# Attention and two feed-forward layers on one core: score jobs that share banks, one job for both products with v, transposes of full width, and another opening

## The chip, the cores and the metric

One core of a Trainium2 chip runs the whole program. The metric is the device time of one execution in microseconds (us), taken as a median of several runs. Five engines work side by side, each through its own list of instructions in order: TensorE (PE, with its weight loads PEld), VectorE (DVE), ScalarE (ACT), GpSimd (POOL) and SyncE (SP), which issues nearly all DMA transfers. TensorE writes into eight PSUM banks of 128 x 512 floats, and VectorE and ScalarE empty them.

## The reference

Four batches of eight heads, 576 positions of 64 numbers:

```
scores = q @ k.T / 8                         (per head, 576 x 576)
cum    = cumsum(log(clip(f, 1e-4, 1)))       (per head, 576)
scores = where(above the diagonal, -1e9, scores + cum[i] - cum[j])
attn   = softmax(scores);  x = attn @ v      -> x: 2304 tokens x 512
h = x @ w_in;   g = h * clip(h + 3, 0, 6) / 6;   x2 = g @ w_out      (512 -> 2048 -> 512)
h = x2 @ w_in2; g = softplus(h);                 out = g @ w_out2
```

## The kernel before

**Stages.** The four big products of the two feed-forward layers run one after the other. The first (step_g, "G", line 965) runs beside the attention, the other three (step_c line 1213, step_a line 1069, step_b line 1268) run alone, on seven products instead of eight of half size. A float32 value is split there in a high and a low part of TensorE's faster type, so one product is three matmuls. The matmuls of the attention are plain float32.

**Attention.** Two heads make a pair; there are 16 pairs, four to a batch. For each pair:

- Raw q and k come by DMA in the tiles qr and kr (load_qk, line 527), and VectorE turns them (qk_job, line 563). For the very first pair this is done head by head.
- decays() computes the running sum of log f for all heads, stores a scaled copy to dec_dram (lines 770, 771), and each later pair gets its two rows broadcast to 128 partitions in the tiles w (line 568). The first pair's rows are spread by TensorE (first_decays, line 583). GpSimd then writes a large number above the diagonal of each 128-wide block of w (hide, line 624).
- The queries are cut in five tiles, CUT: tile 0 has 64 rows, the tiles 1 to 4 have 128, and tile t needs as many key columns as its last row. s_job (line 609) is one **score job** ("S"): the matmuls of one row of S_JOBS for both heads. Five jobs a pair; tiles 1 and 0 share a bank, tile 4 takes two jobs.
- VectorE adds w to the scores out of the bank, takes the row minimum (least, line 631) and writes the tile p; ScalarE takes the exponential and its sum (line 640).
- inv_job takes the inverse of all ten sums at once (lines 654, 655) and scales the ten tiles (fit, line 662).
- t_job (line 690, "T") turns 128 x 128 blocks of p, four jobs a head, one bank each; blocks of tile 0 are 64 rows high and give 64 columns. ScalarE copies the bank to the tiles pt (line 712).
- pv_job (line 737, "V") multiplies with v; two jobs, one for the query columns 320 to 576 and one for 0 to 320, one bank each. ScalarE and VectorE write the result as high and low part (lines 749, 750) into MX, where G reads it.

The pairs' tiles are in two sets (index z), the probabilities in four (p, pb, pc, pd).

**What sets the order.** Nothing is scheduled by the hardware. The program first records every piece of work (op) with its cost, its due time `at` and what it reads and writes; Work.order then plays the engines forward with those costs, gives each engine the ready piece with the least due time, deals out the banks, and emits the instructions in that order. The due times come from the table PLAN. G matmuls are thus dealt in between S, T and V, three or more at a time. Both first-layer weights and later ones pass through staging tiles st: loaded (line 843), converted by ScalarE and VectorE (lines 863 to 867), split (lines 947, 948). The first such load waits for the stored decays (`["dec"]` in weights_g).

The core of the score job:

```python
for ti, a, c, o, q0, r, y, lead, last in todo:
    for h in heads:
        nc.tensor.matmul(bank[bks[h, y].i][:, o:o + c - a], T["Q"][z][h * D:h * D + D, q0:q0 + P],
                         T["K"][z][h * D:h * D + D, a:c], start=lead, stop=last, skip_group_check=True)
```

Of the kernel before, what the change touches and what calls it, by code (L numbers as in the profile page):

```python
# [13 lines left out]
P = 128  # L14
# [6 lines left out]
S_JOBS = [[[(4, 0, 288)]], [[(4, 288, 576)]], [[(3, 0, 448)]], [[(2, 0, 320)]], [[(1, 0, 192), (0, 0, 64)]]]  # L21
# [30 lines left out]
    pc=658.575,  # L52
    pp=2838.384,
    pv=205.16,
    bend=[0.997, 1.008, 0.963, 0.815],
    b0=46.727,
    T0=62.991,
    D1=93.866,
    D2=78.328,
    D3=63.878,  # L60
    D4=62.724,
    gap=14.813,
    gap2=18.0,
    gap3=23.877,
    cA=1.049,
    SA=4.93,
    SC=5.336,
    SB=2.063,
    iva=12.955,
    nwarm=18,  # L70
    sp=0.252,
    evb=0.144,
    u0=8.176,
    u1=53.717,
    u2=4.715,
    u3=-39.214,
    fx=-1.569,
    ul=20.0,
    c1=53.569,
    c2=18.268,  # L80
    c3=11.259,
    cvw=0,
    ldw=91.154,
    xa=26.079,
    xs=-4.984,
    ga=1.976,
    tsp=-12.9,
    fit=7.316,
    xat=22.311,
    xl=4.236,  # L90
    rel=29.77,
    wfrom=5.061,
    lv0=9.944,
    lq1=16.782,
    decst=4.817,
    capH=5,
    capA=7,
    eps=0,
    slp=0,
    slv=0,  # L100
    lat=2.539,
# [16 lines left out]
class Work:  # L118
# [45 lines left out]
    def order(self, caps, eps, slack, lat):  # L164
# [9 lines left out]
        ham = {"w": 0, "act": {}, "warm": False}  # L174

# [42 lines left out]
        while len(out) < len(ops):  # L218
            best = None
            for e in self.ENGINES:  # L220
# [24 lines left out]
                _, s, o = min((c for c in cand if c[0] <= low + eps), key=lambda c: (c[2].at, c[0]))  # L245
# [5 lines left out]
            cost = next(wy[1] for wy in o.ways if wy[0] == e)  # L251
            for wy in o.ways:
                ready[wy[0]].remove(o)
# [48 lines left out]
def attention_two_moe_kernel(  # L302
# [188 lines left out]
    op(("pool", 500, lambda: make_identity(nc, ident)), w=["ident"])  # L491
    op(("dve", 8, lambda: nc.vector.memset(half, 0.5)), w=["half"])
# [22 lines left out]

    def load_qk(nm, b, hp, at, heads=(0, 1)):

        wk.mark = ()
        src = {"qr": q, "kr": k}[nm]

        first = nm == "kr" and (b, hp) == (0, 0)
        eng = nc.scalar if first else nc.sync

        def go():
            for h in heads:
                for g in range(0, D, 32):
                    eng.dma_start(
                        out=raws[nm][h * D + g:h * D + g + 32].rearrange("s (n d) -> s n d", d=32),
                        in_=src[b, 2 * hp + h, :, g:g + 32].rearrange("(n s) d -> s n d", s=32),
                    )  # L530

        n = len(heads)
        dma(go, n * S * D * 4 * 2, 2 * n, 560.0, "act" if first else "sp", w=[(nm, h) for h in heads], at=at, name="load " + nm, from_=at - K["rel"])
# [21 lines left out]
    def qk_job(b, hp, nm, at):  # L555
# [5 lines left out]
        for hs in [(0,), (1,)] if pn == 0 else [(0, 1)]:  # L561
            a, c = hs[0] * D, hs[-1] * D + D
            op(("dve", 726.0, lambda a=a, c=c: nc.vector.transpose(T[x][z][a:c], raws[nm][a:c])), part=(a, a),
               r=[(nm, h) for h in hs], w=[(x + "T", z, h) for h in hs], at=at - (pn == 0 and a == 0), name="T" + x)
# [24 lines left out]

    def s_job(pn, i, idx, at):  # L590
# [7 lines left out]
        need = [(x, z, h) for x in ("QT", "KT") for h in heads]  # L598
        todo = []
# [6 lines left out]
        def go():  # L606
            for ti, a, c, o, q0, r, y, lead, last in todo:
                for h in heads:
                    nc.tensor.matmul(  # L609
                        bank[bks[h, y].i][:, o:o + c - a], T["Q"][z][h * D:h * D + D, q0:q0 + P], T["K"][z][h * D:h * D + D, a:c],  # L610
                        start=lead, stop=last, skip_group_check=True,
                    )

        cost = sum(1.667 * (x[2] - x[1]) + 12 for x in todo) + 200
        op(("pe", cost, go), rows=0.8, seq="S",
           r=need, w=list(bks.values()), banks=list(bks.values()), at=at, name=f"S{pn}.{i}{idx}",
           after=[("P", sets[h], x[0]) for x in todo for h in heads])
        for ti, a, c, o, q0, r, y, _, _ in todo:
            for h in heads:
                par, bk = sets[h], bks[h, y]  # L620
                if c == q0 + r:
# [25 lines left out]
    def inv_job(pn, at):  # L647
# [5 lines left out]
        def inv():  # L653
            nc.vector.tensor_scalar(iv[pn % 2], sv[:, 1], 1e-9, None, op0=ALU.add)
            nc.vector.reciprocal(iv[pn % 2], iv[pn % 2])

        op(("dve", 340, inv), r=[("st", pn % 2, h, t) for h in range(2) for t in range(n)], w=[("iv", pn % 2)], at=at, name="inv")
        for h in range(2):
            for t, (q0, r) in list(enumerate(CUT))[::-1]:
# [4 lines left out]
                op2(("dve", dve(q0 + r, True), fit), r=[("iv", pn % 2)], w=[("P", set_of(pn, h), t)], at=at + 0.1 * (4 - t) + h * K["fit"], name=f"fit{t}")  # L664

    def t_job(pn, i, idx, at):
# [19 lines left out]
        def go():  # L686
            acc = bank[bk.i]
            for p0, ti, k0 in blocks:
                r = CUT[ti][1]
                nc.tensor.transpose(acc[:, p0:p0 + r], T["P"][par][ti][0:r, k0:k0 + P], ident[0:r, 0:r])  # L690

        op(("pe", sum(109.0 if CUT[b[1]][1] == P else 55.0 for b in blocks), go), r=list(rd), w=[bk], banks=[bk], at=at, name=f"TP{idx}",
# [26 lines left out]
    def pv_job(b, hp, idx, at):  # L719
        pn = b * HP + hp  # L720
        z = pn % 2
        y = z
        wk.mark = ()
        bk = Bank(att_banks, "a")
        a, c = V_JOBS[idx]
        rd = [("vr", z)]
        for jobs in T_JOBS:
            for j, ta, tcc in jobs:
                if ta < c and tcc > a:
                    rd += [("PT", i, j, ta - KCUT[j][0]) for i in range(2)]  # L730
        todo = [(i, j, max(a, KCUT[j][0]) - KCUT[j][0]) for j in V_ORDER[idx] for i in range(2)]

        def go():
            acc = bank[bk.i]
            for n, (i, j, s) in enumerate(todo):
                k0 = KCUT[j][0]
# [674 lines left out]
```

## Time and profile before

| | us |
|---|---|
| median of 3 runs | 949.13 |
| lowest and highest run | 947.28, 950.8 |
| the profiled execution, its own time | 948.23 |
| its span, first to last instruction | 946.4 |
| TensorE busy | 927.0 (98%) |
| VectorE busy | 733.3 (77%) |
| ScalarE busy | 538.0 (57%) |
| GpSimd busy | 110.0 (12%) |

The mean granted TensorE clock is 0.993 of full speed. The page's chain of work that ended last, followed back from the end, is 90% TensorE. Stages by time: attention with G from the start to 331 us, G alone to 403, then step_c to 583, step_a to 762 and step_b to the end. A busy TensorE is not one at its peak: matmul ends are modelled, and matmuls overlap. How long a job really holds the engine is read from the chain of waits, whose pieces follow one another without overlap.

### The profile page before, as it was taken

How to read it: one execution, taken by the hardware profiler on the slowest of the kernel's cores; microseconds unless marked ns; L12 is line 12 of the kernel's file. 1: busy time of each engine (PE TensorE's matmuls, PEld its weight loads, DVE VectorE, ACT ScalarE, POOL GpSimd, SP SyncE). 2: the span in 40 equal slices, each digit the busy share in tenths (PEclk: the TensorE clock that was granted, in tenths of full speed). 3: DMA queues.
4: the chain of work that ended last, by engine and by line, in shares of the span. 5: the costliest groups of instructions: out<-in, count | busy, mean ns of one | idle time of the engine just before them, and what ended most of it. 6: DMA issues, size and time to landing. Idle time of an engine off the chain costs nothing.

```text
span 946.4 us, 18694 instructions
## 1 busy us (share of the span) xinstructions
PE 927.0 (98%) x6756; PEld 824.4 (87%) x6756; DVE 733.3 (77%) x1696; ACT 538.0 (57%) x1090; POOL 110.0 (12%) x241
## 2 busy tenths in 40 slices
PE   5999999999999999999999999999999999999998
PEld 4666766777677788899999999999999999999998
DVE  7878977766777468688898799978645888888785
ACT  5868866666677555443354355777567754333332
POOL 3322221111111011102002102100001100000000
PEclk9999999999999999999999999999999999999999
DMA  9957768788666688444534365798624544543442
GB/s 185 184 143 171 208 170 215 203 230 222 173 214 206 200 283 281 155 151 147 172 111 156 113 181 174 267 369 303 240 101 156 190 155 133 154 133 117 133 135 67
DMA packets 196973, 172.76 MB, mean 183 GB/s; under 512 B 103504, under 2 KB 147792, under 8 KB 196880
## 3 DMA queue, kind: packets, MB, share of 16 engines
q1 hardware_dynamic: 194512, 171.27, 61.6%
q8 instruction: 53, 0.87, 0.4%
q10 hardware_dynamic: 2368, 0.30, 0.3%
q14 instruction: 40, 0.33, 0.1%
HBM read 111.68 MB, written 59.84 MB: 181 GB/s over the span
## 4 chain that ended last, share of the span: by engine, by line
PE 90%; DVE 3%; DMA 3%; issue 2%; POOL 1%; ACT 1%; DVEq 0%; POOLq 0%; ACTq 0%
PE bank L965 22%; PE bank L1268 19%; PE bank L1213 19%; PE bank L1069 15%; PE bank L690 6%; PE bank L609 5%; PE bank L737 4%; DMA st<-in_moe_w_out_dram 1%; DMA g_dram<-HY 1%; DMA st<-in_moe_w_in_dram 1%; DMA w<-dec_dram 0%; DVE p L662 0%; DMA wf_dram<-st 0%; POOL w L624 0%; DMA st<-wf_dram 0%
## 5 line engine op out<-in xcount | busy, mean ns | idle before, releaser
L1268 PE MATMUL bank<-U,MX 128*128 128x256 f32 x1512 | 179.9, 281 | 0.0
L1268 PEld LDWEIGHTS bank<-U,MX 128*128 128x128 f32 x1512 | 179.6, 189 | 0.0
L965 PE MATMUL bank<-MX,U 128*128 128x512 f32 (+1 forms) x768 | 177.5, 376 | 0.0
L1213 PE MATMUL bank<-XO,U 128*128 128x256 f32 x1344 | 159.3, 280 | 0.0
L1213 PEld LDWEIGHTS bank<-XO,U 128*128 128x128 f32 x1344 | 158.5, 189 | 0.1
L965 PEld LDWEIGHTS bank<-MX,U 128*128 128x128 f32 x768 | 124.8, 188 | 25.1 <-issue 4.4
L1069 PE MATMUL bank<-MX,U 128*128 128x288 f32 x672 | 91.5, 296 | 0.1
L1069 PE MATMUL bank<-XO,U 128*128 128x288 f32 x672 | 91.2, 296 | 0.0
L1069 PEld LDWEIGHTS bank<-MX,U 128*128 128x128 f32 x672 | 90.2, 188 | 0.5 <-ACT HY L1085 0.3
L1069 PEld LDWEIGHTS bank<-XO,U 128*128 128x128 f32 x672 | 90.3, 188 | 0.0
L624 POOL TENSOR_SCALAR_AFFINE_SELECT w<-w 128x128 f32<-128x128 f32 (+1 forms) x160 | 54.9, 348 | 224.3 <-DVE stats L631 149.5
L970 ACT ACTIVATE HY<-bank,half 128x512 f32<-128x512 f32 x80 | 50.7, 643 | 53.2 <-PE bank L965 46.0
L1166 ACT ACTIVATE MX<-GR 128x768 fp32r<-128x768 f32 x36 | 30.4, 845 | 86.8 <-PE bank L1268 50.4
L971 DVE SCALAR_TENSOR_TENSOR HY<-HY,bank 128x512 f32<-128x512 f32 x80 | 49.5, 628 | 35.3 <-ACT HY L970 34.8
L1088 DVE TENSOR_TENSOR HY<-HY,bank 128x288 f32<-128x288 f32 x96 | 43.1, 451 | 40.1 <-PE bank L1069 39.0
L712 ACT ACTIVATE pt<-bank 128x448 f32<-128x448 f32 (+2 forms) x128 | 59.7, 498 | 21.4 <-PE bank L690 19.8
L1085 ACT ACTIVATE HY<-bank 128x288 f32<-128x288 f32 x128 | 50.6, 408 | 35.8 <-PE bank L1069 34.8
L1166 ACT ACTIVATE XO<-GR 128x768 fp32r<-128x768 f32 x36 | 30.4, 843 | 67.4 <-PE bank L1213 45.1
L609 PE MATMUL bank<-KT,QT 64*128 64x288 f32 (+4 forms) x384 | 59.4, 419 | 6.8 <-DVE stats L631 3.6
L1170 DVE TENSOR_TENSOR MX<-GR,MX 128x768 fp32r<-128x768 f32 x36 | 34.4, 957 | 29.5 <-ACT MX L1166 29.5
L609 PEld LDWEIGHTS bank<-KT,QT 64*128 64x128 f32 x384 | 32.1, 185 | 28.1 <-issue 10.4
L938 DVE TENSOR_TENSOR U<-st,U 128x1024 fp32r<-128x1024 f32 (+1 forms) x48 | 53.6, 1130 | 3.8 <-ACT U L935 3.8
(153 smaller groups left out, 1454.8 us busy)
## 6 DMA issues: line engine op xcount, KB each, us to landing
GR<-g_dram SPq DMA_DIRECT2D x72, 512.0 KB, 3.8
g_dram<-HY SPq DMA_DIRECT2D x32, 576.0 KB, 3.6
st<-in_moe_w_in_dram SPq DMA_DIRECT2D x32, 512.0 KB, 4.8
g_dram<-HY SPq DMA_DIRECT2D x64, 256.0 KB, 3.2
st<-in_moe_w_out_dram SPq DMA_DIRECT2D x32, 512.0 KB, 5.2
wf_dram<-st SPq DMA_DIRECT2D x48, 256.0 KB, 3.6
st<-wf_dram SPq DMA_DIRECT2D x48, 256.0 KB, 3.1
w<-dec_dram SPq DMA_DIRECT2D x30, 288.0 KB, 5.0
```

Of the source, the lines that this page charges most:

```text
L609: nc.tensor.matmul(bank[bks[h, y].i][:, o:o + c - a], T["Q"][z][h * D:h * D + D, q0:q0 + P], T["K"][z][h * D:h * D + D, a:c], start=lead, ...
L624: nc.gpsimd.affine_select(out=blk, in_=blk, compare_op=ALU.is_ge, fill=-1e9 / scale, base=0, pattern=[[-1, r]], channel_multiplier=1)
L690: nc.tensor.transpose(acc[:, p0:p0 + r], T["P"][par][ti][0:r, k0:k0 + P], ident[0:r, 0:r])
L712: e.activation(out=place(i, j, a, c), in_=src(), func=ACTF.Copy)
L938: e.tensor_tensor(to(1), src(), to(0).bitcast(F32), op=ALU.subtract)
L965: nc.tensor.matmul(bank[bk.i][:, 0:n], w, x, start=(c == 0 and y == 0), stop=(c == NC - 1 and y == 2))
L970: op(("act", act(n, True, 1) + 10, lambda: nc.scalar.activation(out=g, in_=bank[bk.i][:, 0:n], func=ACTF.Relu, scale=1.0 / 6.0, bias=half) ...
L1069: nc.tensor.matmul(bank[bks[b].i][:, 0:HA], wa[u][:, c], xa[v][:, c], start=(nm in ("P1", "P2", "P5") and c == 0 and y == 0), stop=(c == 1 ...
L1085: op(("act", act(HA, True) + 30, lambda: nc.scalar.activation(out=to(q), in_=bp(), func=ACTF.Copy)), r=new, banks=[ba], w=[("H", i, q)], a ...
L1166: op(("act", act(cnt, False), lambda src=src, dst=dst: nc.scalar.activation(out=dst(0), in_=src(), func=ACTF.Copy)), r=rd, w=[("gf", m, i, ...
L1213: nc.tensor.matmul(bank[bks[b].i][:, o * 256:(o + 1) * 256], *ops, start=(p == 0 and o == 0 and y == 0), stop=(p == NPR - 1 and y == 2), s ...
L1268: nc.tensor.matmul(bank[bks[b].i][:, o * 256:(o + 1) * 256], ga[u], wa[v], start=(p == 0 and o == 0 and y == 0), stop=(p == NPR - 1 and y ...
```

## The change

- **Score jobs share banks.** S_JOBS has four jobs instead of five: tile 0 goes into tile 3's bank, tile 1 into tile 2's. Tile 0's minimum is taken after the next job (late_rows).
- **They stand together.** Work.order gets a bonus `stick`: after a score job or a product with v, TensorE prefers another of the same kind; it also charges each change of kind on TensorE (`turn`).
- **One job for both products with v**, with two banks.
- **Transposes of full width**: blocks of tile 0 are turned with all 128 rows (64 of them zeros), and the next block overwrites the surplus columns.
- **First masks by TensorE**: for the first pair the large number is added by matmuls of the identity with a tile `bar`, ten in all, and GpSimd's ten selects on w fall away.
- **Raw q, k and decays sooner**: the second pair's q and k land in two tiles p that are still free, so they need not wait for the first pair's; the first sum of decays is due sooner; weights no longer wait for it.
- For the first four pairs the inverse is taken in two parts, tiles 3 and 4 first.
- Nearly every number of PLAN is another one. They are due times, margins and penalties, and no work.

```diff
-S_JOBS = [[[(4, 0, 288)]], [[(4, 288, 576)]], [[(3, 0, 448)]], [[(2, 0, 320)]], [[(1, 0, 192), (0, 0, 64)]]]
+S_JOBS = [[[(4, 0, 288)]], [[(4, 288, 576)]], [[(3, 0, 448), (0, 0, 64)]], [[(2, 0, 320), (1, 0, 192)]]]
...
-    capH=5,
+    capH=4,
-    slp=0,
+    slp=139.65,
+    stick=11.647,
...
+                same = last if e == "pe" and last in ("S", "V") else ""
+                _, s, o = min((c for c in cand if c[0] <= low + eps), key=lambda c: (c[2].at - (stick if same and kind_of(c[2]) == same else 0.0), c[0]))
...
+    bar = ap.tile([P, P], F32, name="bar")
+    op(("pool", 346, lambda: nc.gpsimd.affine_select(out=bar, in_=bar, compare_op=ALU.is_ge, fill=-1e9 / scale, base=0, pattern=[[-1, P]], channel_multiplier=1)), w=["bar"])
...
+    def raw(nm, pn, heads):
+        if pn == 1:
+            y = 2 + (nm == "kr")
+            return T["P"][y][4][:, 0:S], [("P", y, 4)]
+        return raws[nm], [(nm, h) for h in heads]
...
+            for ti, a, c, o, q0, r, y, lead, last in todo if barred else ():
+                if c == q0 + r:
+                    for h in heads:
+                        nc.tensor.matmul(bank[bks[h, y].i][:, o + q0 - a:o + c - a], ident, bar[:, 0:r], start=False, stop=last, skip_group_check=True)
...
+        if idx == 2:
+            late_rows.append(rest.pop())
+        elif idx == 3:
+            rest.append(late_rows.pop())
...
+        for t0, t1 in ((3, n), (0, 3)) if pn < 4 else ((0, n),):
...
-                nc.tensor.transpose(acc[:, p0:p0 + r], T["P"][par][ti][0:r, k0:k0 + P], ident[0:r, 0:r])
+                nc.tensor.transpose(acc[:, p0:p0 + P], T["P"][par][ti][:, k0:k0 + P], ident)
...
-        bk = Bank(att_banks, "a")
-        a, c = V_JOBS[idx]
+        bks = [Bank(att_banks, "a") for _ in V_JOBS]
...
-        raw_weights(i, 0, 0, ft, at, ["dec"] * (ft == 0))
+        raw_weights(i, 0, 0, ft, at)
```

The numbers of PLAN tell a reader nothing; the order that comes out of them does. Three places of it follow, as lists of instructions (line, operation, written tile, read tiles, size). bank_69 to bank_76 are the eight banks.

TensorE's list at the last two score jobs of a pair of the third batch, before (KT and QT are the turned k and q; L690 turns blocks of p):

```order
L609 MATMUL bank_73<-KT_174,QT_172 128x320
L609 MATMUL bank_76<-KT_174,QT_172 128x320
L690 MATMUL bank_74<-ident,p_158 128x64
L690 MATMUL bank_74<-ident,p_159 128x128
L690 MATMUL bank_74<-ident,p_160 128x128
L609 MATMUL bank_75<-KT_174,QT_172 128x192
L609 MATMUL bank_69<-KT_174,QT_172 128x192
L609 MATMUL bank_75<-KT_174,QT_172 128x64
L609 MATMUL bank_69<-KT_174,QT_172 128x64
L965 MATMUL bank_70<-MX,U_192 128x512 x3
```

and at the last two score jobs of a pair of the same batch now:

```order
L636 MATMUL bank_73<-KT_173,QT_171 128x448
L636 MATMUL bank_75<-KT_173,QT_171 128x448
L636 MATMUL bank_73<-KT_173,QT_171 128x64
L636 MATMUL bank_75<-KT_173,QT_171 128x64
L1005 MATMUL bank_74<-MX,U_195 128x512 x3
L636 MATMUL bank_76<-KT_173,QT_171 128x320
L636 MATMUL bank_69<-KT_173,QT_171 128x320
L636 MATMUL bank_76<-KT_173,QT_171 128x192
L636 MATMUL bank_69<-KT_173,QT_171 128x192
```

Tile 0 (64 columns) now stands behind tile 3 in its bank and tile 1 behind tile 2; blocks of p_158, tile 0, are turned elsewhere, as 128x128.

TensorE's list where the two products with v of one pair meet, before:

```order
L737 MATMUL bank_76<-pt_181,vr_185 64x64
L737 MATMUL bank_76<-pt_184,vr_185 64x64
L965 MATMUL bank_70<-MX,U_191 128x512 x3
L737 MATMUL bank_73<-pt_179,vr_185 64x320
L737 MATMUL bank_73<-pt_182,vr_185 64x320
```

and now:

```order
L775 MATMUL bank_70<-pt_181,vr_185 64x64
L775 MATMUL bank_70<-pt_184,vr_185 64x64
L775 MATMUL bank_71<-pt_179,vr_185 64x320
L775 MATMUL bank_71<-pt_182,vr_185 64x320
L775 MATMUL bank_71<-pt_180,vr_185 64x192
```

The G matmuls that stood between the two products are gone from there, and two banks are held at once.

SyncE's list from its first transfer on, before (p, qr, kr, vr: raw f, q, k, v; st: weights; w: decays):

```order
L763 DMA p_162<-in_f_dram 32x576
L527 DMA qr<-in_q_dram 32x18x32 x4
L545 DMA vr<-in_v_dram 128x4x64 x2
L547 DMA vr<-in_v_dram 64x2x64
L843 DMA st_188<-in_moe_w_in_dram 128x4x256
L843 DMA st_189<-in_moe_w_in_dram 128x4x256
L527 DMA kr<-in_k_dram 32x18x32 x4
L527 DMA qr<-in_q_dram 32x18x32 x4
L771 DMA dec_dram<-w_178 32x576
```

and now:

```order
L803 DMA p_162<-in_f_dram 32x576
L549 DMA qr<-in_q_dram 32x18x32 x4
L549 DMA kr<-in_k_dram 32x18x32 x2
L549 DMA pc<-in_q_dram 32x18x32 x4
L549 DMA pd<-in_k_dram 32x18x32 x4
L811 DMA dec_dram<-w_178 32x576
L567 DMA vr<-in_v_dram 128x4x64 x2
L569 DMA vr<-in_v_dram 64x2x64
L567 DMA vr_185<-in_v_dram 128x4x64 x2
L569 DMA vr_185<-in_v_dram 64x2x64
L549 DMA qr<-in_q_dram 32x18x32 x4
L590 DMA w_177<-dec_dram 128x576
```

The second pair's q and k (pc, pd) and the decays' store have moved ahead of v and of every weight load; the first broadcast of decays, 28th transfer in the list before, is the 27th.

## Rows read from the trace of the kernel before

**Rows 1.** Busy time by stretch: start:end, length, engines, granted clock, DMA share, GB/s.

```profile
10.00:60.00 50.00, 37.95 (x252) 26.12 (x253) 41.68 (x148) 36.29 (x105) 16.26 (x39) 0.90 0.92 185
15.00:20.00 5.00, 0.86 (x5) 0.30 (x4) 4.66 (x19) 4.63 (x16) 2.09 (x7) 0.92 0.86 203
20.00:25.00 5.00, 2.07 (x10) 2.10 (x11) 4.90 (x16) 2.54 (x9) 0.96 (x2) 0.50 1.04 192
60.00:400.00 340.00, 339.82 (x2071) 250.59 (x2068) 250.97 (x738) 218.44 (x544) 52.54 (x132) 1.00 0.73 206
403.00:946.00 543.00, 538.88 (x4381) 538.23 (x4379) 432.99 (x799) 278.10 (x435) 35.56 (x34) 1.00 0.52 168
```

**Rows 2.** Who waited for whom, TensorE: us in total, times, longest.

```profile
PE bank L690 <- DVE p L662: 4.0, 1, 4.0
PE bank L609 <- DVE stats L631: 3.6, 4, 2.0
```

**Rows 3.** Chain of work that ended last, steady part: start, us, instructions.

```profile
129.74 1.98 PE bank L609 x12
131.72 0.89 PE bank L965 x3
...
138.31 0.57 PE bank L690 x3
138.88 0.69 PE bank L965 x3
139.58 0.69 PE bank L609 x4
140.26 1.59 PE bank L965 x6
141.86 1.89 PE bank L737 x20
143.74 0.90 PE bank L965 x3
144.64 1.13 PE bank L737 x12
145.77 0.90 PE bank L965 x3
146.66 0.44 PE bank L690 x4
147.10 0.70 PE bank L965 x3
...
204.46 5.60 PE bank L965 x24
...
328.38 2.87 PE bank L737 x32
```

**Rows 4.** Instructions in order of time, opening: start, us, engine, what, idle before.

```profile
10.73 0.76 PE L609 MATMUL bank<-KT,QT 64*128 64x288 f32 x4
11.63 0.46 DVE L631 CUSTOM_DVE_ANT_0 p<-bank,w 128x288 f32<-128x288 f32 x1 [0.45 <-POOL w L624]
...
19.43 1.62 SPq L568 DMA_DIRECT2D w<-dec_dram  x2
...
24.94 0.44 DVE L631 CUSTOM_DVE_ANT_0 pc<-bank,w 128x288 f32<-128x288 f32 x1
```

**Rows 5.** DMA issues on the page: KB each, median us from issue to landing.

```profile
w<-dec_dram SPq DMA_DIRECT2D x30, 288.0 KB, 5.0
```

**Rows 6.** VectorE busy by line, 0 to 340: lines 631, 662, 563, 750 in turn.

```profile
0.00:340.00 340.00, 79.09 (x384) 0.98 0.76 195
...
0.00:340.00 340.00, 51.71 (x160) 0.98 0.76 195
...
0.00:340.00 340.00, 25.96 (x34) 0.98 0.76 195
...
0.00:340.00 340.00, 15.15 (x44) 0.98 0.76 195
```

More of the change, by code (lines that the diff above doesn't have):

```diff
@@ L51 @@
 PLAN = dict(
[L52 to L69, printed above, removed]
-    nwarm=18,
[L71 to L77, printed above, removed]
-    ul=20.0,
[L79 to L95, printed above, removed]
-    capH=5,
+    pc=770.465,
+    pp=618.104,
+    pv=0,
+    bend=[1.174, 1.0, 1.0, 0.812],
+    b0=61.02,
+    T0=64.024,
+    D1=95.58,
+    D2=78.67,
+    D3=91.919,
+    D4=85.876,
+    gap=16.562,
+    gap2=9.508,
+    gap3=28.322,
+    cA=1.253,
+    SA=5.158,
+    SC=5.58,
+    SB=2.457,
+    iva=9.099,
+    nwarm=18,
+    sp=0.599,
+    evb=-0.046,
+    u0=-5.516,
+    u1=15.018,
+    u2=2.565,
+    u3=17.82,
+    fx=4.03,
+    ul=20.0,
+    c1=16.714,
+    c2=24.399,
+    c3=40.164,
+    cvw=2.987,
+    ldw=39.661,
+    xa=-29.983,
+    xs=1.49,
+    ga=1.536,
+    tsp=-0.82,
+    fit=-2.043,
+    xat=10.863,
+    xl=5.136,
+    rel=26.422,
+    wfrom=6.221,
+    lv0=13.973,
+    lq1=11.142,
+    decst=-2.554,
+    capH=4,
     capA=7,
     eps=0,
-    slp=0,
+    slp=139.65,
     slv=0,
-    lat=2.539,
+    stick=11.647,
+    lat=2.081,
 )
@@ L251, in order @@
             cost = next(wy[1] for wy in o.ways if wy[0] == e)
+            if e == "pe":
+                cost += turn.get((last, kind_of(o)), 0.0)
+                last = kind_of(o)
             for wy in o.ways:
@@ L519, in load_qk @@
         src = {"qr": q, "kr": k}[nm]
-        first = nm == "kr" and (b, hp) == (0, 0)
+        dst, keys = raw(nm, b * HP + hp, heads)
+        first = nm == "kr" and (b, hp) == (0, 0) and 0 in heads
         eng = nc.scalar if first else nc.sync
@@ L532, in load_qk @@
         n = len(heads)
-        dma(go, n * S * D * 4 * 2, 2 * n, 560.0, "act" if first else "sp", w=[(nm, h) for h in heads], at=at, name="load " + nm, from_=at - K["rel"])
+        dma(go, n * S * D * 4 * 2, 2 * n, 560.0, "act" if first else "sp", w=keys, at=at, name="load " + nm, from_=at - K["rel"])
     cz = 1
@@ L598, in s_job @@
         need = [(x, z, h) for x in ("QT", "KT") for h in heads]
+        barred = pn == 0
+        if barred:
+            need += ["ident", "bar"]
         todo = []
@@ L728, in pv_job @@
             for j, ta, tcc in jobs:
-                if ta < c and tcc > a:
-                    rd += [("PT", i, j, ta - KCUT[j][0]) for i in range(2)]
-        todo = [(i, j, max(a, KCUT[j][0]) - KCUT[j][0]) for j in V_ORDER[idx] for i in range(2)]
+                rd += [("PT", i, j, ta - KCUT[j][0]) for i in range(2)]
+        todo = [[(i, j, max(a, KCUT[j][0]) - KCUT[j][0]) for j in V_ORDER[idx] for i in range(2)] for idx, (a, c) in enumerate(V_JOBS)]
         def go():
-            acc = bank[bk.i]
-            for n, (i, j, s) in enumerate(todo):
-                k0 = KCUT[j][0]
-                nc.tensor.matmul(acc[i * D:i * D + D, s + k0 - a:c - a], T["vr"][z][:, j, i], place(i, j, s, c - k0),
-                                 start=(n < 2), stop=(n >= len(todo) - 2), skip_group_check=True)
@@ L740, in pv_job @@
[L740 to L750 removed]
+            for idx, (a, c) in enumerate(V_JOBS):
+                acc = bank[bks[idx].i]
+                for n, (i, j, s) in enumerate(todo[idx]):
+                    k0 = KCUT[j][0]
+                    nc.tensor.matmul(acc[i * D:i * D + D, s + k0 - a:c - a], T["vr"][z][:, j, i], place(i, j, s, c - k0),
+                                     start=(n < 2), stop=(n >= len(todo[idx]) - 2), skip_group_check=True)
```

75 lines of the change are left out of this document (43 added, 32 removed).

## Prediction

> **What bounds the kernel now.** I read the busy time by stretch first [rows 1]. From 60 us to 400 TensorE is busy 339.82 of 340 us at the full granted clock, and from 403 to the end 538.88 of 543. There only less TensorE time makes the kernel shorter. From 10 to 60 it is different: TensorE is busy 37.95 of 50 us and the clock is at 0.90, while VectorE is busy 41.68. Then the waits [rows 2]: the longest of TensorE's are for the scaled tiles p (4.0 us) and for minima (3.6 us in four), and both lie in the opening. Third, the chain in the steady part [rows 3]. Its pieces do not overlap, so they are the price of each kind of job, which a mean duration of pipelined matmuls is not. Last the opening in order of time [rows 4].
>
> The profiled execution took 948.23 us, 0.9 below the median of 949.13. The sums below are made against it, and 0.9 is added at the end.
>
> **Prices, from [rows 3].** Three G matmuls take 0.69 or 0.70 us after a transpose (24 take 5.60, so 0.233 each), but 0.89 or 0.90 after scores or products with v. So leaving S or V for G costs 0.20. A lone score job of 288 columns takes 0.69, three jobs of 288, 448 and 320 columns together 1.98: the 768 further columns cost 1.29, or 1.68 ns each, 288 of them are worth 0.48, and entering costs 0.21. Each border between S and G is thus about 0.20. The two products with v take 1.89 and 1.13 apart and 2.87 together, with one 0.20 less behind them: a join saves 0.35, or 0.175 for a border between V and G. Four transposes of full height take 0.44, and the job with one block of 64 and two of 128 takes 0.57 where three full ones would take 0.33: the odd block costs 0.24.
>
> **The change on TensorE, 10 us onward.**
>
> - Full transposes: 32 heads have one odd job each, 32 x 0.24 = 7.7 us. Where the job stands behind scores, which use 64 rows too, the switch may be paid anyway; I take 7.0, between 5 and 7.7.
> - Fewer borders. Counted in both lists up to step_c, borders between S and G fall from 58 to 42, between V and G from 40 to 27: 16 x 0.20 + 13 x 0.175 = 5.5 us. Borders of S with T or V fall from 39 to 17. No row prices one alone; they lie between 0 and 0.20, and I take half: 22 x 0.10 = 2.2 (0 to 4.4). Borders of T with G cost nothing in these rows.
> - First masks: ten more matmuls of up to 128 columns. At the price of a full transpose they take 1.1 us, at half of a lone score job each 10 x 0.35 = 3.5. They stand in the opening, where TensorE is idle for 12 us and waits for VectorE; I cost them at nothing, and at 1.1 to 3.5 if that cover goes. GpSimd's ten selects in front of the first minima go with them.
> - One matmul more or less elsewhere: none. G and the three later stages have the same number of matmuls, 543 us from 403 on with 4 us without work. VectorE has 14 more small sums there that GpSimd did, but it is busy 433 of 543 us. I cost them at nothing, and at up to 2 if the first factors of step_c, which stand behind some of these sums in its list, come late.
>
> Sum: 7.0 + 5.5 + 2.2 = **14.7 us less**, bounds 10 to 18.
>
> **The opening.** Before, the first score matmul starts at 10.73 [rows 4]. From 10 to 60 TensorE lacks 12.05 us of being busy, and the clock costs 37.95 x 0.10 = 3.8 [rows 1]. So by 60 us some 26.6 us have gone without work. After that nothing is lost, so this is a fixed cost of the kernel. In the changed list the first G stands behind all score jobs of four pairs, the transposes of three and the products with v of two; before it stood behind three, less than two, and one. The work ahead of it is 4 x 3.0 + 3 x 3.3 + 2 x 2.87 + 1.1 = 28.7 us by the prices above (1600 columns of scores and a border or two; 30 x 0.11; one join).
>
> When can that first G run? Its transposes need the third pair's scaled tiles from VectorE. VectorE's four main lines in the attention come to 79.09 + 51.71 + 25.96 + 15.15 = 171.9 us for 16 pairs [rows 6], 10.7 a pair; that is slower than TensorE's 9.2 or so, so VectorE sets the pace. The second pair's first minimum came at 24.94 [rows 4], after its decays: SyncE issued that broadcast at 19.43, and it lands 5.0 later [rows 5]. It was the 28th transfer and is the 27th. All three weight loads that stood ahead of it are gone, so I put its issue between 16.7 and 18.7 and its landing between 21.7 and 23.7. From 22.7 there are two pairs of VectorE to go, 21.4 us, some 2 us of stops behind exponentials, and 3.3 us of transposes: 49.4. By then 49.4 - 28.7 = 20.7 us are lost instead of 26.6. The gain is **5.9 us**, with bounds of -1 (the fourth pair is late too, and the masks show) and 11 (no stops, broadcast at 21.7, clock full).
>
> The second pair's q and k now go ahead of v and of the weights on SyncE. Behind them wait the first weights, but no G needs these before 49, and the value tiles, which the first product with v needs only behind the scores of three pairs.
>
> Total: 948.2 - 14.7 - 5.9 = 927.6, plus 0.9 for the median: 928.5, said as **929 us**.
>
> **A rule on the clock.** In [rows 1] the granted clock was 0.50 from 20 to 25 us, 1.2 GHz of 2.4, after TensorE had been busy 0.86 us of the five before; with long runs of transposes it then rose again to an average of 0.90 for the whole opening. The Trainium skill, TensorE: Matmul & The Clock Gate, "Part 4: PE-mode transpose", says that the full clock does not engage for transposes, since they do not count as a busy array. By that rule the new opening, without G, would stay at 1.2 GHz. The trace so far speaks against it, so it is only a rival.
>
> **Rivals.**
>
> 1. **The opening gains nothing**: another stop of VectorE, the broadcast or ScalarE takes the place of the shorter wait. For it: VectorE is busy 41.68 of 50 us already. Against it: the weights' conversions leave its list there. 948.2 - 14.7 + 0.9 = 934, or up to 939 if the opening loses 5.
> 2. **Banks hold TensorE** (the other side). Score jobs in a row take up to eight banks, the double product two, and each bank waits for VectorE's minimum. For it: TensorE's 3.6 us of waits for minima, up to 2.0 each [rows 2]. Against it: none of these after the opening, and VectorE has 340 - 251 = 89 us free from 60 to 400 [rows 1]. If each of the 13 pairs behind the opening cost one such wait, 13 x 2.0 = 26 us, and 948.2 - 20.6 + 26 + 0.9 = 955. From 1.6 us a pair on it takes all that is won. The Trainium skill, TensorEngine Tiling (Array Packing), "PSUM Bottleneck", warns of this: a faster TensorE does not speed up the copies out of PSUM. No run here shows it.
> 3. **The clock stays low in the opening.** TensorE stands still between pairs as from 15 to 20 us, and the 90 transposes ahead of the first G run at 1.2 GHz: 90 x 0.11 = 9.9 us more, 938.
> 4. **Full transposes save nothing**, because the switch of height is paid by the neighbours: 7.0 more, 936.
>
> **How the numbers follow.** Forecast 0.60 (its own range, from the bounds of the terms, 920 to 938), rival 1 0.17, rival 2 0.10, rival 3 0.07, rival 4 0.06. About 0.5%, or 4.7 us, is what a measurement of this kernel can tell from no change: faster is under 944.4, slower over 953.9. The forecast and rivals 1, 3 and 4 all end faster; 0.03 of them goes to two mishaps at once. Of rival 2's 0.10 half is over 953.9. That gives 0.87 faster, 0.07 the same, 0.06 slower. The range for 8 in 10 is 918 to 941: the forecast with rivals 1, 3 and 4, leaving out rival 2 and the ends.
>
> **What would show it.** In the chain of the changed kernel: three transposes with tile 0 in 0.33 us instead of 0.57, G behind them in 0.70, the double product in about 2.87, fewer G pieces of 0.90. In the opening: the second pair's first minimum at 22 to 24 us, the first G at 48 to 51, a granted clock over 0.9 between 25 and 50. step_c begins at 382 to 384 instead of 403. From there to the end still 543 us. I am wrong if TensorE shows waits for minima after 60 us, if step_c starts later than 390, or if the last three stages take over 546.

## The result and the profile after

The changed kernel takes **926.17 us** (median of 4 runs, 924.99 to 926.98), the kernel before 949.89 beside it (4 runs, 947.28 to 950.8). The ratio is 0.9754, with a 95% interval of 0.973 to 0.9777. The forecast was 929, with a range of 918 to 941. The profiled execution took 925.79 us, its span 923.6. Lines have moved: G is 1005 now, S 636, T 730, V 775, the masks 643, the minima 669, the scaling 703, step_c 1253.

Busy time by stretch of the changed kernel, columns as in [rows 1]:

```profile
10.00:60.00 50.00, 47.34 (x367) 34.45 (x365) 47.24 (x189) 40.81 (x128) 14.96 (x38) 1.00 0.82 177
15.00:20.00 5.00, 4.54 (x36) 3.28 (x34) 4.24 (x22) 4.39 (x18) 0.57 (x1) 1.00 0.93 202
20.00:25.00 5.00, 4.08 (x32) 3.04 (x31) 4.97 (x20) 2.60 (x6) 1.16 (x5) 1.00 0.96 207
25.00:30.00 5.00, 4.79 (x41) 2.84 (x40) 4.96 (x27) 5.00 (x16) 2.44 (x9) 1.00 0.95 212
30.00:40.00 10.00, 9.61 (x78) 7.04 (x76) 9.92 (x41) 10.00 (x35) 4.32 (x9) 1.00 0.85 159
40.00:60.00 20.00, 19.32 (x158) 14.48 (x154) 19.71 (x75) 17.16 (x53) 6.48 (x16) 1.00 0.71 168
60.00:378.00 318.00, 317.78 (x1989) 247.57 (x1988) 240.54 (x700) 209.73 (x520) 53.99 (x121) 1.00 0.79 221
378.00:923.60 545.60, 541.08 (x4387) 539.52 (x4385) 441.08 (x821) 281.53 (x439) 22.73 (x23) 1.00 0.53 169
```

From 10 to 60 us TensorE is busy 47.34 us instead of 37.95, at a clock of 1.00 instead of 0.90. VectorE, the third busy column, is now full: 4.97 + 4.96 + 9.92 + 19.71 = 39.56 of the 40 us from 20 to 60. ScalarE, the fourth, is as full from 25 to 40 (15.00 of 15), so that in this stretch the rows do not tell which of the two sets the pace.

TensorE's waits of the changed kernel, the longest of those for other engines' work on the attention, columns as in [rows 2]:

```profile
PE bank L636 <- DVE stats L669: 0.7, 1, 0.7
PE bank L730 <- DVE p L703: 0.7, 2, 0.5
PE bank L730 <- DVE p3b L703: 0.5, 1, 0.5
```

All of them lie in the opening. The 4.0 us for p and the 3.6 us for minima [rows 2] have come down to 0.7 each, and a wait of 3.1 us for the second pair's turned q is gone.

The chain that ended last, steady part, columns as in [rows 3]:

```profile
131.91 0.70 PE bank L1005 x3
132.61 0.33 PE bank L730 x3
132.93 0.69 PE bank L1005 x3
...
134.65 1.12 PE bank L636 x8
135.77 0.90 PE bank L1005 x3
...
138.63 2.87 PE bank L775 x32
141.50 2.98 PE bank L1005 x12
...
159.12 2.52 PE bank L636 x20
```

Three transposes with the block of tile 0 take 0.33 us where they took 0.57 [rows 3]. G behind scores still takes 0.90: a border costs what it did, there are fewer of them.

The opening in order of time, columns as in [rows 4]:

```profile
10.77 1.24 PE L636 MATMUL bank<-KT,QT 64*128 64x288 f32 x8
11.68 0.46 DVE L669 CUSTOM_DVE_ANT_0 p<-bank,w 128x288 f32<-128x288 f32 x1 [0.99 <-PE bank L636]
...
15.13 0.97 SPq L590 DMA_DIRECT2D w<-dec_dram  x2
...
21.20 0.46 DVE L669 CUSTOM_DVE_ANT_0 pc<-bank,w 128x288 f32<-128x288 f32 x1
```

The first scores start no sooner (10.73 before). But the broadcast of the second pair's decays is issued at 15.13 instead of 19.43, and its first minimum comes at 21.20 instead of 24.94. The first G starts at 47.82.

What stood in front of that minimum? Before, in order of time, two pieces of VectorE's work on the weights, and GpSimd's first select on the second pair's decays, which had waited for the broadcast:

```profile
20.07 0.69 DVE L948 TENSOR_TENSOR U<-st,U 128x512 fp32r<-128x512 f32 x1 [0.41 <-ACT U L947]
21.35 0.65 DVE L866 SCALAR_TENSOR_TENSOR st<-st 128x512 uint32<-128x512 uint32 x1
24.04 0.94 POOL L624 TENSOR_SCALAR_AFFINE_SELECT w<-w 128x128 f32<-128x128 f32 x1 [4.64 <-DMA w<-dec_dram]
```

and now:

```profile
19.43 0.61 POOL L662 TENSOR_SCALAR_AFFINE_SELECT w<-w 128x128 f32<-128x128 f32 x1 [12.49 <-DMA w<-dec_dram]
21.06 0.19 DVE L695 RECIPROCAL iv<-iv 128x6 f32<-128x6 f32 x1
```

The decays of the pair's first head had landed in both kernels when VectorE came to it, 0.9 us before in the old one and 1.8 us before now, and VectorE had no idle time in front of that minimum in either. So its own list set the moment. Between the first minimum of the first pair (11.63, now 11.68) and the first of the second, it did seven pieces of work on the weights before, 4.1 us, and does none now. It also scaled all ten tiles of the first pair there, and scales four now. From 10 to 60 us the weights took 7.4 us of VectorE, and take 3.9 now; the rest has moved behind the opening, where VectorE has time.

**Where the time went.** I call *work* the TensorE time of all jobs of the attention and G up to a point, by prices fitted to the 113 stretches between two pieces of G in the trace before (they are met to 0.05 us, root mean square), and *lost* the time of that point less the work. Masks count as work. These are estimates: other prices that meet the same stretches as well move the time lost by 60 us by up to 0.8 us and that by step_c by up to 3.

| up to step_c | begins | work | lost | from there to the end |
|---|---|---|---|---|
| before | 403.0 | 375.0 | 28.0 | 543.4 |
| after | 378.5 | 361.9 | 16.6 | 545.1 |

Work fell by 13.1 us, lost time by 11.4, and the rest grew by 1.7. Of the first and the last, 0.35 is only that six narrow G matmuls (256 columns, 0.117 us each) stand behind the first step_c matmul now, where three did. At 60 us the lost time was already 28.4 before and 18.1 after: nearly all of the second part is won in the opening.

### The profile page after: what moved, and what is told of

Its sections match the earlier page's. It is cut to its first block, busy times and chain, and to the rows that moved or that the text cites. A ratio compares the mean times of both kernels' runs of the same rounds, so it can differ in the third digit from the quotient of the medians.

```text
span 923.6 us, 18723 instructions
## 1 busy us (share of the span) xinstructions
PE 914.2 (99%) x6776; PEld 829.1 (90%) x6776; DVE 734.7 (80%) x1718; ACT 535.3 (58%) x1091; POOL 97.4 (11%) x218
## 4 chain that ended last, share of the span: by engine, by line
PE 91%; DVE 3%; DMA 2%; issue 1%; ACT 1%; SPq 1%; POOL 0%; DVEq 0%; POOLq 0%; ACTq 0%
PE bank L1005 21%; PE bank L1308 19%; PE bank L1253 19%; PE bank L1109 16%; PE bank L730 5%; PE bank L636 4%; PE bank L775 4%; DMA qr<-in_q_dram 1%; PE bank L1330 1%; SPq L549 1%; DMA st<-in_moe_w_out_dram 1%; DVE XO L1062 0%; DVE HY L1128 0%; DVE U L978 0%; DMA w<-dec_dram 0%
## 5 line engine op out<-in xcount | busy, mean ns | idle before, releaser
L1005 PE MATMUL bank<-MX,U 128*128 128x512 f32 (+1 forms) x768 | 174.1, 374 | 0.2 <-DVE HY L1011 0.2
L752 ACT ACTIVATE pt<-bank 128x448 f32<-128x448 f32 (+2 forms) x128 | 57.9, 507 | 21.2 <-PE bank L730 20.9
L1128 DVE TENSOR_TENSOR HY<-HY,bank 128x288 f32<-128x288 f32 x96 | 42.5, 451 | 29.6 <-PE bank L1109 27.6
L636 PE MATMUL bank<-KT,QT 64*128 64x288 f32 (+4 forms) x384 | 54.9, 412 | 0.7 <-DVE stats L669 0.7
L636 PEld LDWEIGHTS bank<-KT,QT 64*128 64x128 f32 x384 | 33.6, 186 | 20.7 <-issue 9.6
L906 DVE SCALAR_TENSOR_TENSOR st<-st 128x512 uint32<-128x512 uint32 x64 | 44.1, 688 | 9.6 <-ACT st L903 6.9
```

The lines of the kernel that those rows point to most:

```text
L752: e.activation(out=place(i, j, a, c), in_=src(), func=ACTF.Copy)
L1005: nc.tensor.matmul(bank[bk.i][:, 0:n], w, x, start=(c == 0 and y == 0), stop=(c == NC - 1 and y == 2))
```

## The experiments

Each kernel was run beside the kernel before (948.5 to 949.3 us there, 949.89 beside the changed kernel). "More" and "less" stand against the 926.17 us of the changed kernel unless said otherwise, and are good to about 1.5 us. Times within a run are those of one profiled execution. The first scores start there between 9.73 and 11.01 us, at 10.77 in the changed kernel, and up to 1.0 us sooner in runs 1, 3 and 4, which have its opening; differences of 1 us in the opening therefore tell nothing. Where an edit changes more than a cost, the planner deals the list out anew, so that work and lost time both move; the table at the end keeps them apart.

**1. Half-height transposes again.**

```diff
-                nc.tensor.transpose(acc[:, p0:p0 + P], T["P"][par][ti][:, k0:k0 + P], ident)
+                r = CUT[ti][1]
+                nc.tensor.transpose(acc[:, p0:p0 + r], T["P"][par][ti][0:r, k0:k0 + P], ident[0:r, 0:r])
```

> The changed kernel with half-height transposes again for the tiles of 64 rows; the list of instructions stays the same otherwise. Theory (the odd block costs 0.24 us, once in each of 32 heads): 926.2 + 7.0 = 933.2 us, between 931.2 and 933.9; in the chain three transposes with the odd block take 0.57 instead of 0.33, step_c begins at 384 to 386 instead of 378.5. Rival (the neighbours pay for the switch of height anyway): 926.2 us, less than 1 us away.

Measured: 930.62 us, 4.4 more; step_c at 383.8. In the chain, at the same place of the list:

```profile
134.08 0.57 PE bank L731 x3
134.65 0.69 PE bank L1006 x3
```

The price in the chain is as forecast, 0.24 us for an odd job. But the sum is under the theory's range of 931.2 to 933.9. Only 24 of the 32 lie behind 60 us: 24 x 0.24 = 5.8, and step_c moved by 5.3. Whether the other eight, in the opening, cost nothing because TensorE waits for VectorE there is not shown: the lost time went down by 0.9 as the work went up, but the first scores started 0.7 us sooner in this execution.

**2. Full transposes alone, in the kernel before** (the same two lines the other way round).

> The kernel before with full-width transposes alone; its list of instructions stays the same otherwise. Theory: 949.9 - 7.0 = 942.9 us, between 942.2 and 944.9, and step_c at 395 to 398 instead of 403. Rival (the switch is paid anyway): 949.9 us. A second rival (what is won is lost again to waits for VectorE in the opening): between the two, with step_c at 399 or later.

Measured: 942.14 us, 7.2 less than 949.3 beside it (ratio 0.9923, 0.9908 to 0.9938); step_c at 396.1, 6.9 sooner. The theory held, a little below its range, and the fourth rival fell.

**3. The ten masks twice.**

```diff
-                        nc.tensor.matmul(bank[bks[h, y].i][:, o + q0 - a:o + c - a], ident, bar[:, 0:r], start=False, stop=last, skip_group_check=True)
+                        for d in range(2):
+                            nc.tensor.matmul(bank[bks[h, y].i][:, o + q0 - a:o + c - a], ident, bar[:, 0:r], start=False, stop=last and d == 1, skip_group_check=True)
```

> The changed kernel with each of the ten first mask matmuls done twice (the mask is added twice; the rest and its order stay). Theory of the forecast (the masks lie in TensorE's idle time of the opening): 926.2 us, within 0.7. Rival (the opening is now bound by TensorE, busy 47.34 of its 50 us, so that masks show in full): 1.1 to 3.5 us more, 927.3 to 929.7.

Measured: 926.73 us, 0.56 more (925.82 to 928.2). The list holds 1.1 us more work, and 0.6 less was lost by step_c. The theory's 0.7 held, but the rival's 1.1 lies within the spread, and the first scores started 1.0 us sooner in this execution, so that whether the masks are covered is not settled. The second pair's first minimum came at 22.33 here, 1.1 us later than in the changed kernel, at no clear cost.

**4. No stick** (`stick=0`).

> The changed kernel with the planner's stick at 0, so that a score job or a product with v no longer draws its like behind it. In the list, borders between S and G rise from 42 to 72, V and G fall from 27 to 23, S with T or V rise from 17 to 23; the work ahead of the first G stays the same. Theory (0.20, 0.175 and 0.10 us a border): 6.0 - 0.7 + 0.6 = 5.9 us more, 932.1, all of it after 60 us, with more G pieces of 0.89 in the chain. Rival (borders are covered by other waits): 926.2, within 1 us.

Measured: 930.35 us, 4.2 more. step_c begins 5.8 us later, 0.7 of which is six narrow G matmuls that now stand ahead of it. That leaves 5.1 for the borders, against 5.9. They are real. Whether my prices for them were a little high is not settled: the first scores started 1.0 us sooner in this execution.

**5. The second pair's q and k in the first pair's tiles** (`if pn == 1` in raw() never true).

> The changed kernel with the second pair's q and k in the tiles of the first pair again, so that they load only after the first transposes have read these; its list is planned anew, with 359.1 us of priced TensorE work up to step_c instead of 361.6. Theory (the early q and k bring the decays' broadcast and the second pair's first minimum forward, which was worth 3.7 us): that minimum at 24 to 26 us instead of 21.2, some 3 to 7 us more lost by 60 us, and 926.2 - 2.5 + 3 to 7 = 927 to 931. Rival (VectorE sets the pace wherever q and k stand, nothing more is lost): 923.7.

Measured: 936.13 us, 10 more, although the list has 2.5 us less work. The second pair's first minimum came at 24.45. The broadcast was issued only 1.3 us later than in the changed kernel (16.39) and had landed by 20.8, so it is not what held this pair. VectorE was again without idle time in front of that minimum: from the first minimum on it had done 2.4 us of work on the weights, whose first loads went out at 6.21 instead of 20.68, and all ten scalings. The pair's scores were late too. They started at 20.66 instead of 16.89, and at half the clock:

```profile
20.66 4.10 PE L636 MATMUL bank<-KT,QT 64*128 64x288 f32 x16 [0.73 <-ACT pt L752]
24.95 2.45 PE L636 MATMUL bank<-KT,QT 64*128 64x320 f32 x8 [0.19 <-DVE stats L669]
```

```profile
20.00:25.00 5.00, 4.15 (x17) 2.78 (x17) 4.96 (x14) 1.21 (x4) 1.95 (x3) 0.50 0.99 207
```

The same sixteen took 2.16 us in the changed kernel. And the delay does not end at 60 us. TensorE's waits from 60 to 400 in this run:

```profile
PE bank L775 <- DVE stats L669: 3.5, 2, 1.9
PE bank L730 <- DVE p3b L703: 1.7, 1, 1.7
```

Why the pairs behind the opening wait as well is not shown; I take it that the plan deals out their work for a VectorE that is further on. The theory gave the sign, but named the broadcast, and had only about half of the size: the delay is paid as idle time, at the clock, and once more in the pairs behind the opening.

**6. Every edit of the opening undone** (edits 5, 7 and 11 together, and the factors in one part).

> The changed kernel with every edit of the opening undone (second pair's q and k in the old tiles, first masks by GpSimd's selects, first weights behind the decays, the factors in one part), the rest as it is; its list has 357.8 us of priced work up to step_c instead of 361.6. Theory (these edits give the opening's gain): 28 us lost by 60 us as in the kernel before, 926.2 - 3.8 + 10 = 932. Rival (the gain comes from the planner's new numbers): 17 to 18 us lost as in the changed kernel, 922.4.

Measured: 940.55 us, 14.4 more; 27.4 us lost by 60 us as in the kernel before, 33.3 by step_c. Against the changed kernel that is 9.3 us more by 60 us and 16.7 by step_c; the last stages take 3.4 more, and the work is 3.9 less. Together the opening's edits make the opening's gain; the new numbers do not make it without them. From 15 to 20 us TensorE does nothing, waiting 6.2 us for the second pair's turned k:

```profile
15.00:20.00 5.00, 0.00 (x0) 0.00 (x0) 4.84 (x20) 4.98 (x19) 2.41 (x5) 0.76 0.78 129
```

**7. The first masks by GpSimd's selects.**

```diff
-        barred = pn == 0
+        barred = False
-                if c == q0 + r and pn:
+                if c == q0 + r:
```

> The changed kernel with the first pair's masks by GpSimd's selects again, as before; 360.7 us of priced work up to step_c instead of 361.6. Theory (the masks on TensorE are covered, and so are the selects): 925.3 to 926.2. Rival 1 (the first minima wait for the selects, which come at 1 to 2 us apart): 1 to 3 us more lost, 926.5 to 928.5. Rival 2 (masks on TensorE delay the second pair): 923 to 924.5.

Measured: 929.15 us, 3.0 more, above the range of rival 1 and further still from the theory. The second pair's minimum came even sooner (19.70). But 1.8 us more were lost by 60 us: from 15 to 20 us TensorE was busy 2.56 us instead of 4.54, at a clock of 0.82. Another 3.1 us came in the last three stages, on which more below. The work, 1.2 us less, takes some of it back. Up to step_c this kernel is only 0.7 us behind, so the run does not show that masks on TensorE are worth 3 us.

**8. The planner's new numbers alone, in the kernel before.**

> The kernel before with the planner's new numbers alone (no stick, no new jobs, old opening); 374.6 us of priced work up to step_c instead of 375.0. Theory (the numbers alone are worth nothing): 949.5, within 2. Rival (the numbers, which put the weights and the first G elsewhere, make the opening's gain): 28 us lost become 18, 939 to 940. Second rival (numbers that suit the new jobs hold these up): 955 or more, with waits of TensorE after 60 us.

Measured: 954.76 us, 6.2 more than the kernel before beside it (ratio 1.0055, 1.0036 to 1.0073), between the theory and the second rival. By 60 us 29.6 us are lost, by step_c 32.0, and the last stages take 547.7. The numbers are no gain by themselves.

**9. More stick** (`stick=40`).

> The changed kernel with the planner's stick at 40 instead of 11.6. In its list borders between S and G fall from 42 to 27, V and G from 27 to 26, S with T or V from 17 to 10; the work ahead of the first G stays the same to 0.2 us. Theory (0.20, 0.175 and 0.10 us a border): 3.0 + 0.2 + 0.7 = 3.9 us less, 922.3. Rival (longer rows of score jobs fill the banks and TensorE waits for minima): waits after 60 us and 926 or more.

Measured: 924.75 us, 1.4 less (ratio to before 0.9742, 0.9727 to 0.9756, which overlaps that of the changed kernel). The work fell by 2.6 although the six narrow G now stand ahead of step_c, 3.3 for the jobs alone against the 3.9 of the theory. But 2.7 more were lost by step_c, in new waits such as this one for a part of the weights:

```profile
106.89 1.18 PE L1005 MATMUL bank<-MX,U 128*128 128x512 f32 x4 [1.68 <-DVE U L988]
```

It is no wait for minima, as the rival had it, but a wait all the same. Fewer borders pay only as long as every other piece stays in time. The 1.4 us are not settled by these runs.

**10. The old jobs** (five score jobs with the old S_JOBS, two products with v; the stick and full transposes stay).

> The changed kernel with five score jobs and two products with v for each pair again, full transposes, stick and opening as they are; planned anew, 363.0 us of priced work up to step_c instead of 361.6, and 39.7 us of work ahead of the first G instead of 29.8. Theory (the new jobs count only by the borders that they save): 926.2 + 1.4 = 927.6. Rival 1 (smaller jobs free their banks sooner, and less is lost): 924 to 926. Rival 2 (the larger stretch without G stands still for VectorE): 930 or more, with over 20 us lost by 60 us.

Measured: 936.72 us, 10.5 more. The time is rival 2's, its reason is not: by 60 us 18.9 us are lost, about as much as in the changed kernel. TensorE's waits from 60 to 400 show where it went, at the entry to step_c:

```profile
PE bank L1250 <- issue: 4.6, 1, 4.6
PE bank L1250 <- DVE U L975: 1.1, 1, 1.1
```

The second names a factor of step_c; for the first the profile shows no releaser. The last stages take 2.2 us more. Plan and jobs changed together here, so this run does not price the new jobs.

**11. The dependency between the first weights and the decays** (`["dec"] * (ft == 0)` back in weights_g).

> The changed kernel with the first weights waiting for the decays in DRAM again, and nothing else; the plan moves the decays' store behind more loads on SyncE (broadcast from the 13th row to the 19th), and its priced work up to step_c is 359.3 us instead of 361.6. Theory (the broadcast is what the second pair waits for): its first minimum at 25 us or later instead of 21.2, lost time up by 4 to 10 us as in the run with q and k in the old tiles, 928 to 934. Rival (the broadcast has room): 923.9.

Measured: 946.37 us, 20 more, for one dependency. It works the other way round than the expectation and the description of the kernel before say. `Work.op` makes a reader wait only for a writer that is recorded already (`if t in self.writer`), and the program records weights_g before decays(). So the first load of weights waits for nothing, and the store of the decays, recorded later, must stand behind this load, as it writes what the load is said to read. SyncE's order shows it: the first weights go out at 18.09 and the store at 23.00 in this run, at 5.81 and 13.53 in the kernel before; without the dependency, in the changed kernel, the store goes out at 8.74 and the weights at 20.68.

The broadcast follows at 27.11. Here, and in no other run, VectorE does wait for the decays: it is idle from 28 to 30 us, 6.2 us in all since the first minimum, and takes up the second pair with them:

```profile
32.63 0.46 DVE L669 CUSTOM_DVE_ANT_0 pc<-bank,w 128x288 f32<-128x288 f32 x1 [0.58 <-DMA w<-dec_dram]
```

TensorE then stands still too, and comes back at half the clock:

```profile
24.00:26.00 2.00, 1.29 (x10) 0.80 (x8) 1.51 (x4) 1.74 (x5) 0.00 (x0) 1.00 0.92 128
...
28.00:30.00 2.00, 1.36 (x7) 0.65 (x3) 0.00 (x0) 0.00 (x0) 0.00 (x0) 0.50 1.01 297
30.00:33.00 3.00, 0.00 (x0) 0.00 (x0) 1.49 (x3) 1.31 (x2) 0.29 (x1) 0.50 0.94 238
```

```profile
33.15 3.37 PE L636 MATMUL bank<-KT,QT 64*128 64x288 f32 x8 [3.79 <-DVE stats L669]
37.25 4.99 PE L775 MATMUL bank<-pt,vr 128*64 128x256 f32 x32 [0.73 <-DVE stats L669]
```

Eight score matmuls take 3.37 us against 1.24 at full clock, the double product 4.99 against 2.94. The theory held, beyond its range.

**12. The steady part undone, the opening kept** (edits 1 and 10, `stick=0`, no turn costs).

> The changed kernel with everything of the steady part undone (half-height transposes, five score jobs, two products with v, no stick and no turn costs in the planner) and every edit of the opening kept. Its list has 377.7 us of priced work up to step_c instead of 361.6; borders between S and G 72 instead of 42, V and G 42 instead of 27, S with T or V 37 instead of 17. Theory (steady part and opening add up): 17 to 18 us lost by 60 us as in the changed kernel, 926.2 + 16.1 = 942, between 939 and 945. Rival (the early opening needs the new jobs and falls back without them): over 25 us lost by 60 us, and 950 or more.

Measured: 944.29 us, 18.1 more; 17.3 us lost by 60 us; step_c at 395.9, 17.4 later. Opening and steady part do add up: the early opening doesn't need the new jobs. Against the kernel before, this one is only 4.5 us faster (948.77 beside it, ratio 0.9953, 0.9936 to 0.9969), although some 10 us less are lost by step_c: its list holds 2.7 us more work, and the last stages take 1.7 us more.

All of it in one table, in the order of the second pair's first minimum (times in us; "lost by 60" is read at the first piece of G from 58 us on, in run 5 at 66.8):

| kernel | second pair's first minimum | lost by 60 | lost by step_c | work | median |
|---|---|---|---|---|---|
| 7 masks by GpSimd | 19.70 | 19.9 | 18.5 | 360.7 | 929.15 |
| 12 steady part old | 20.29 | 17.3 | 18.2 | 377.7 | 944.29 |
| 10 old jobs | 20.36 | 18.9 | 23.7 | 363.1 | 936.72 |
| 9 stick 40 | 21.13 | 18.3 | 19.3 | 359.3 | 924.75 |
| after | 21.20 | 18.1 | 16.6 | 361.9 | 926.17 |
| 6 opening old | 23.94 | 27.4 | 33.3 | 358.0 | 940.55 |
| 5 raw q, k old | 24.45 | 25.7 | 30.9 | 359.2 | 936.13 |
| before | 24.94 | 28.4 | 28.0 | 375.0 | 949.89 |
| 8 new numbers alone | 25.71 | 29.6 | 32.0 | 374.6 | 954.76 |
| 11 weights and decays | 32.63 | 30.2 | 38.7 | 359.4 | 946.37 |

Two groups stand apart. Where that minimum comes by 21.2 us, 17 to 20 us are lost by 60; where it comes at 24 or later, 26 to 30. VectorE's list divides them in the same way: in the first five kernels no work on the weights stands between the first pair's first minimum and this one, in the other five 2.4 to 4.7 us of it. Runs 5, 6, 8 and 11 each change several of these things together, since the planner deals out the lists anew. What one of them is worth by itself, no run shows.

## Why the prediction was right

**Full transposes** (forecast 7.0): right in the kernel before. The price of 0.24 us was read correctly, and run 2 got 7.2 for the 32. In the changed kernel undoing them cost 4.4 (run 1), under the bounds of 5 to 7.7; why it was less is open.

**Borders** (forecast 5.5 and 2.2): right. The work fell by 13.1 us. The masks add 1.1 to it, and 0.35 of G moved behind the first step_c, so the jobs alone got 13.1 + 1.1 - 0.35 = 13.8 us cheaper against a forecast of 14.7. Less the 7 of the transposes, about 7 are left for borders where I had 7.7. Run 4 has 5.1 for 5.9. Neither difference is larger than what the estimates leave open. The bounds, 10 to 18, held.

**Masks** (forecast 0): not settled. Twice the masks cost 0.56 us (run 3), which excludes neither 0 nor the 1.1 of their price. Without them it is worse by 3.0 (run 7), but nearly all of that came in the last stages.

**The opening** (forecast 5.9, bounds -1 to 11): this term was mis-sized. Lost time fell from 28.4 to 18.1 us by 60, so the gain is 10.3, less the masks' 1.1 that stand in the work: about 9. On the same footing the forecast was 4.8: the masks' 1.1 stand in the 28.7 us of work ahead of the first G, and so lower the 20.7 lost, but the sum of the work leaves them out. Three things were off. First, the 26.6 us lost before came from busy time, which counts a pipelined matmul at its modelled length; by prices it was 28.4. Second, I put the first G at 49.4, with 20.7 us lost, and it came at 47.82 with 18.0. I had allowed VectorE some 2 us of stops behind exponentials; but from 20 to 60 us it is busy 39.56 of 40. VectorE does set the pace there, as the step said, with ScalarE as full from 25 to 40, and it is fed without a stop. The minimum came at 21.20, 0.8 ahead of the 22 to 24 that I gave, and the broadcast at 15.13, ahead of 16.7 to 18.7. Third, the step had the wait wrong: it took the broadcast for what the second pair waits for. In both kernels the decays had landed before VectorE came to that pair, and what let it come sooner is the 4.1 us of work on the weights and the six scalings that no longer stand ahead. I had named the weights' conversions only against the first rival, and had put no time on them. That the minimum fell near my range is therefore in part luck: the landing moved by 4.6 us, VectorE's own list by 3.7. Run 11 shows that the broadcast can hold the pair, if it comes late enough.

**The later stages** (forecast 0, up to 2): 1.7 us longer, 0.35 of it the moved G. Most of the rest is in stops: six of over 40 ns behind the first step_c matmul before, 0.7 us together; sixteen now, 1.9 us.

**The signs.** step_c begins at 378.5, sooner than the 382 to 384 named, and the minimum and the first G (47.82, not 48 to 51) a little sooner than their ranges; what I had called wrong (waits for minima after 60, step_c after 390, over 546 us for the last stages) didn't come. The opening gave some 3 us more than the 5.9 in the sum, the steady part 0.9 less and the last stages took 1.4 more, so that errors in part cancel: that 926.17 lies so near to 929 is partly luck.

**Rivals.** The first (no gain in the opening) fell: in run 6, without the opening's edits, 9.3 us more are lost by 60 us. The second (banks hold TensorE) fell: no wait for minima after 60 us in the changed kernel, and none over 0.7 us ahead of it. But what the Trainium skill says in TensorEngine Tiling (Array Packing), "PSUM Bottleneck", that a faster TensorE does not speed up the copies out of PSUM, agrees with the opening now in part: VectorE is the full engine there, 39.56 of 40 us, but about half of this, 19.7 us of minima and low parts, reads PSUM. The third (a cold clock) fell in this kernel, with 1.00 in every stretch, though it is part of what the late openings pay: runs 5 and 11 show 0.50. The rule of the Trainium skill, TensorE: Matmul & The Clock Gate, "Part 4: PE-mode transpose", would have kept the opening at 1.2 GHz; the trace does not agree. In run 11 TensorE ran nothing but transposes from 19.44 to 27.20, with stops, and was granted 1.00 all that time. Transposes alone even raised a clock that had fallen, in the kernel before:

```profile
18.22 0.76 PE L609 MATMUL bank<-KT,QT 64*128 64x288 f32 x4 [3.12 <-DVE QT L563]
22.93 3.48 PE L690 MATMUL bank<-ident,p 128*128 128x128 f32 x15 [3.96 <-DVE p L662]
26.34 2.69 PE L609 MATMUL bank<-KT,QT 64*128 64x288 f32 x20
```

```profile
19.30:26.00 6.70, 3.07 (x14) 2.65 (x14) 6.26 (x23) 3.87 (x12) 2.06 (x3) 0.50 1.04 187
26.10:28.90 2.80, 2.80 (x22) 1.78 (x22) 1.96 (x7) 1.30 (x3) 0.83 (x4) 1.00 0.98 275
```

Behind the score matmuls, which end at 18.98, there are only these fifteen transposes up to 26.34; the granted clock is 0.50 up to 26.00 and 1.00 from 26.10. The fourth rival fell in run 2, and in run 1 the transposes cost 4.4 us.

**Left open.** The last three stages have the same matmuls in every kernel here, yet take 543.3 to 548.5 us: in runs 6, 7 and 8 some 5 to 6 us of stops, up to 1.05 us each, most of them inside step_a. I take it that they go with how the plan deals VectorE's sums out, but no run takes one plan's late part alone. Why the planner puts work on the weights ahead of the second pair in some lists and not in others is also open, and with it what each of the opening's edits is worth.

## What to carry to other kernels

Price jobs by the chain, where pieces do not overlap, and count borders between kinds of job, and odd shapes, in both lists; such a sum came within about 1 us of what the traces give here. Where another engine sets the pace of an opening, read what that engine does ahead of the work that counts, besides what it waits for: here work on weights stood in front that G needed only behind 43 us. With a second pair that starts some 4 us sooner went about 9 us less lost time, because a late one is paid as idle time, as half a clock and in some lists once more as waits behind the opening. A dependency holds in the order in which the pieces are recorded, so check in the list which way it acts. A planner's numbers need not carry over: in the old kernel they cost 6 us.

## What the runs showed of the hardware

- Half the clock stretched the plain float32 jobs by 1.7 to 2.7: sixteen score matmuls 2.16 to 4.10 us, eight 1.24 to 3.37 (with a wait for a bank among them, which these rows do not part from the clock), the double product 2.94 to 4.99.
- A single transpose of a 64-row block among 128-row ones costs 0.24 us more than a full one in the chain, and 0.22 on average over the 32 of run 2, although it moves half the data.
- The granted clock kept 1.00 through transposes with stops from 19.44 to 26 us in run 11, and fell only behind 26 us (0.95 from 26 to 28, 0.50 from 28 on). In the kernel before it rose from 0.50 to 1.00 at 26 us, when TensorE had run only transposes since 18.98.
